# The last group of second experts, the slots' outputs, the combination and the output transfers by halves of the columns

## The chip, the cores and the metric

One Trainium2 chip, one of its cores. The metric is the device time of one execution in microseconds, the median of several runs.

## What is computed

Three layers in a row, all in float32 at the outside. Causal attention with a decay (4 x 8 heads, 576 rows, 64 columns), a mixture of 4 dense experts on the 2304 x 512 result, and a second, soft mixture, which the change touches:

```python
logits = x @ phi                       # 2304 x 32 slots
d = softmax of logits over the rows
slot_input = d.T @ x                   # 32 x 512, 8 experts of 4 slots
for e in range(8):
    h = np.maximum(slot_input[e] @ w1[e], 0.0)   # 4 x 1024
    slot_out[e] = h @ w2[e]                       # 4 x 512
c = softmax of logits over the slots
return c @ slot_out                    # 2304 x 512
```

## The kernel before, in words

Attention and the first mixture take the first 930 us or so. They stay as they are, instruction for instruction, and so does the order that the kernel's own scheduler makes of them. What follows is written out by hand, from L2096 on, in one straight line for all engines; each engine runs its own instructions in the order of the program.

The second experts are worked in two groups of four (`for g in range(NG2)`, L2158). Of a group, `ffn_in` (L2127) does the first layer, 1024 columns in two pieces of 512; `ffn_tr` (L2138) transposes; `ffn_out` (L2144) does the second layer: for each of eight blocks `m` of the inner dimension, the four experts write four strips of 32 partitions of one PSUM bank, `fo`. In the trace a float32 matmul is two rows, so a block `m` is eight. The weights come in through pages of SBUF: `fill` (L1837) starts the transfer of the next weights from SP into pages that are free, and `used` frees a page behind its matmul. The last weights are under way when group 1's second layer begins.

A group's result is scaled by the slots' totals on ScalarE into `so[g]` (L2175), and VectorE takes its largest magnitude (L2176). The slots' outputs are then `sel` times `so`: `sel[:, 0]` for group 0 (L2171, placed between the blocks of group 1) and `sel[:, 1]` for group 1 (L2183), summed in the bank `so`. For float16 they are scaled by a power of two that comes from the largest value of all: `spread` (L446) brings the 128 maxima of the partitions into every partition by a matmul, `top` (L449) takes the maximum of a row, two integer steps (L2188, L2190) make the power of two, ScalarE writes `SO` in float16 (L2192), VectorE puts the rounding rest into its lower half (L2193) and folds the scale into the factor of each row, `rc` (L2195).

Then the combination, for 18 tiles of 128 rows: one float16 matmul of 512 columns (L2199), an eviction with the factor of the row, by ScalarE for even tiles (L2204) and by VectorE for odd ones (L2202), and the transfer of 128 x 2 KB from SP (L2206). Tiles 4 and 13 hold 64 rows each of two sequences, so they go in two transfers of 64 rows: 20 in all. Each tile has a page of its own in SBUF.

Of the kernel before, what the change touches and what calls it, by code (L numbers as in the profile page):

```python
# [12 lines left out]
I32 = mybir.dt.int32  # L13
AF = mybir.ActivationFunctionType
ALU = mybir.AluOpType
AX = mybir.AxisListType
# [10 lines left out]
C_MUL = 1024.0  # L27
PAIRS = (0, 3, 3, 2)
PLAIN = (0, 1, 0, 0)
T_SO = 13  # L30
BIG = float(2 ** 23)
# [253 lines left out]
def moe_attention_kernel(ctx: ExitStack, tc: tile.TileContext, q, k, v, f, probs, w1, w2, phi, s1, s2, out):  # L285
    nc = tc.nc
    B, H, S, D = q.shape
    NT, DM = out.shape
# [4 lines left out]
    KD, KF = DM // 128, F // 128  # L293
    NTILE = NT // 128
# [10 lines left out]
    def page(p, n=1, dt=F32):  # L305
        a = arena[:, p * 512:(p + n) * 512]
        return a if dt is F32 else a.bitcast(dt)
# [63 lines left out]
    dyn = Pages(range(nxt[0], NPAGE))  # L371
# [25 lines left out]
    def rows(u):  # L397
        b, i = units[u]
        if i:
            return [(0, b * S + 64 + 128 * (i - 1), 128)]  # L400
        return [(0, b * S, 64), (64, (b + 1) * S, 64)]
# [43 lines left out]
    def spread(ps, col):  # L445
        nc.tensor.matmul(out=ps[:, 0:128], lhsT=col.to_broadcast([128, 128]), rhs=ident, start=True, stop=True)  # L446

    def top(dst, ps):
        nc.vector.tensor_reduce(out=dst, in_=ps[:, 0:128], axis=AX.X, op=ALU.max)  # L449
# [1207 lines left out]
    with tc.manual_schedule():  # L1657
# [65 lines left out]
        def bank(name):  # L1723
            if not ps2:
                return ps_m.tile([128, 512], F32, tag="m", name=name)
            return ps2[0].tile([128, 512], F32, tag="b", name=name)
# [25 lines left out]
        T = sc.task  # L1752
# [56 lines left out]
        sel = gp[:, E2 * 32:512].rearrange("p (g c) -> p g c", g=2)  # L1809
# [15 lines left out]
        NG2 = E2 // 4  # L1825
# [9 lines left out]
        where, held = {}, {}  # L1835

        def fill(keep=0):  # L1837

            ps = sorted(dyn.free_at, key=lambda p: (dyn.free_at[p], p))
            ps = sorted(ps[:max(0, len(ps) - keep)])  # L1840
            while ps and stream:
                ty, e2, n, kk = stream[-1]
                x = 1
                while (x < len(ps) and x < len(stream) and ps[x] == ps[0] + x
                       and stream[-1 - x] == (ty, e2, n, kk + x)):
                    x += 1
                if ty == "a":
                    src = s1[e2, kk * 128:(kk + x) * 128, n * 512:(n + 1) * 512]
                else:
                    src = s2[e2, kk * 128:(kk + x) * 128, :]  # L1850
                nc.sync.dma_start(out=page(ps[0], x).rearrange("p (k n) -> p k n", k=x),
                                  in_=src.rearrange("(k p) n -> p k n", p=128))
                for y in range(x):
                    key = stream.pop()
                    p = ps.pop(0)
                    where[key], held[key] = page(p), p
                    del dyn.free_at[p]

        def used(key):
            dyn.free(held.pop(key))  # L1860


        cT = page(dyn.alloc(3), 3, F16)[:, 0:NTILE * 128].rearrange("p (t c) -> p t c", c=128)
        x2T_p = dyn.alloc(3)
        x2T = page(x2T_p, 3).rearrange("p (k c) -> p k c", k=KD)
        mix = page(dyn.alloc(1))
# [4 lines left out]
        rc = mix[:, 404:404 + NTILE]  # L1871
        run_nm = [mix[:, 424:425], mix[:, 425:426]]
        run_sum = mix[:, 426:427]
        st_ = mix[:, 432:448]
# [132 lines left out]
        j = NBLK - 1  # L2007
# [61 lines left out]
        pm = bank("mg")  # L2069
# [19 lines left out]
        hs, so = page(hT_p, 2), [page(hT_p + 4), page(hT_p)]  # L2089
        hT = page(hT_p + 2, 2).rearrange("p (m c) -> p m c", m=KF)  # L2090
        SO = page(x2T_p + 2, 1, F16)[:, 0:DM]
# [4 lines left out]
        p = bank("sT")  # L2096
        for kk in range(KD):
            nc.tensor.matmul(out=p[:, kk * NS:(kk + 1) * NS], lhsT=slotS[R3, kk * 128:(kk + 1) * 128], rhs=G96[R3],
                             start=True, stop=True)
# [27 lines left out]
        def ffn_in(g, n, p, ks):  # L2127
            for kk in ks:
                for j in range(4):
                    key = ("a", 4 * g + j, n, kk)  # L2130
                    nc.tensor.matmul(out=p[32 * j:32 * j + 32, :], lhsT=slT[:, kk, 4 * g + j, :],  # L2131
                                     rhs=where[key], start=(kk == 0), stop=(kk == KD - 1))
                    used(key)
                fill(0)
            if ks[-1] == KD - 1:
                nc.scalar.activation(out=hs[:, n * 512:(n + 1) * 512], in_=p, func=AF.Relu)

        def ffn_tr(m0):  # L2138
            p = bank("hT")
            for m in range(4):  # L2140
                nc.tensor.transpose(p[:, m * 128:(m + 1) * 128], hs[:, (m0 + m) * 128:(m0 + m + 1) * 128], ident)
            nc.scalar.activation(out=hT[:, m0:m0 + 4, :], in_=p.rearrange("p (m c) -> p m c", m=4), func=AF.Copy)

        def ffn_out(g, p, ms):  # L2144
            for m in ms:
                for j in range(4):
                    key = ("b", 4 * g + j, 0, m)
                    nc.tensor.matmul(out=p[32 * j:32 * j + 32, :], lhsT=hT[:, m, 32 * j:32 * j + 32],  # L2148
                                     rhs=where[key], start=(m == 0), stop=(m == KF - 1))
                    used(key)  # L2150
                fill(0)

        def late():
            for x in tails.pop(0) if tails else ():
                x()

        pS = bank("so")
        for g in range(NG2):  # L2158
            ps = [bank("fh") for _ in range(NH)]
            ffn_in(g, 0, ps[0], range(KD))  # L2160
            late()
            ffn_in(g, 1, ps[1], range(KD // 2))
            ffn_tr(0)
            ffn_in(g, 1, ps[1], range(KD // 2, KD))
            p = bank("fo")
            ffn_out(g, p, range(2))
            ffn_tr(4)
            late()
            ffn_out(g, p, range(2, KF - 2))
            if g == NG2 - 1:  # L2170
                nc.tensor.matmul(out=pS, lhsT=sel[:, 0, :], rhs=so[0], start=True, stop=False)  # L2171
            ffn_out(g, p, range(KF - 2, KF))
            late()
            r = st_[:, 14 + g:15 + g]
            nc.scalar.activation(out=so[g], in_=p, func=AF.Copy, scale=r)  # L2175
            nc.vector.tensor_reduce(out=st_[:, 10 + g:11 + g], in_=so[g], axis=AX.X, op=ALU.max, apply_absolute_value=True)  # L2176
            if g == 0:
                nc.vector.tensor_scalar(out=st_[:, 10:11], in0=st_[:, 10:11], scalar1=float(2.0 ** -90), scalar2=None,
                                        op0=ALU.max)
                nc.vector.tensor_scalar(out=rc, in0=csum, scalar1=1e-9, scalar2=None, op0=ALU.add)  # L2180
                nc.vector.reciprocal(out=rc, in_=rc)
        p = pS
        nc.tensor.matmul(out=p, lhsT=sel[:, 1, :], rhs=so[1], start=False, stop=True)  # L2183
        nc.vector.tensor_tensor(out=st_[:, 11:12], in0=st_[:, 10:11], in1=st_[:, 11:12], op=ALU.max)
        pm = bank("mp")
        spread(pm, st_[:, 11:12])
        top(st_[:, 12:13], pm)
        nc.vector.tensor_scalar(out=st_[:, 12:13].bitcast(I32), in0=st_[:, 12:13].bitcast(I32), scalar1=0x7F800000,  # L2188
                                scalar2=None, op0=ALU.bitwise_and)
        nc.vector.tensor_scalar(out=st_[:, 13:14].bitcast(I32), in0=st_[:, 12:13].bitcast(I32), scalar1=-1.0,  # L2190
                                scalar2=(254 + T_SO) * BIG, op0=ALU.mult, op1=ALU.add)
        nc.scalar.activation(out=SO, in_=p, func=AF.Copy, scale=st_[:, 13:14])  # L2192
        nc.vector.scalar_tensor_tensor(out=SO[64:128], in0=p[64:128], scalar=st_[64:128, 13:14], in1=SO[64:128],  # L2193
                                       op0=ALU.mult, op1=ALU.subtract)
        nc.vector.tensor_scalar(out=rc, in0=rc, scalar1=st_[:, 12:13], scalar2=float(2.0 ** -T_SO) / C_MUL,  # L2195
                                op0=ALU.mult, op1=ALU.mult)
        for T in range(NTILE):
            p = bank("out")
            nc.tensor.matmul(out=p, lhsT=cT[:, T, :], rhs=SO, start=True, stop=True)  # L2199
            o = page(dyn.alloc(1))  # L2200
            if T % 2:
                nc.vector.tensor_scalar(out=o, in0=p, scalar1=rc[:, T:T + 1], scalar2=None, op0=ALU.mult)  # L2202
            else:
                nc.scalar.activation(out=o, in_=p, func=AF.Copy, scale=rc[:, T:T + 1])  # L2204
            for p0, r0, n in rows(T):
                nc.sync.dma_start(out=out[r0:r0 + n, :], in_=o[p0:p0 + n])  # L2206


DBG = {}
# [27 lines left out]
```

## Time and profile before

| | |
|---|---|
| median of 3 runs | 991.23 us (990.97 to 993.67) |
| profiled execution | 991.54 us |
| its span, first to last instruction | 989.8 us |
| instructions | 20653 |
| TensorE busy | 943.2 us, 95% |
| VectorE busy | 577.3 us, 58% |
| ScalarE busy | 471.9 us, 48% |
| GpSimd busy | 324.1 us, 33% |
| granted TensorE clock, mean | 0.992 |

Busy times are sums over the span; what a change at one place is worth is read at that place, in the chain that ended last and in the queues' own rows. The span leaves out the 1.7 us by which the execution's own time is longer.

### The profile page before, as it was taken

The numbers are of one execution on the slowest core, as the hardware profiler recorded it, in microseconds if no ns is written. First come the engines' busy times: TensorE is split into PE (matmuls) and PEld (weight loads), VectorE is DVE, ScalarE is ACT, GpSimd is POOL, SyncE is SP. The second block draws the span as 40 slices with busy tenths as digits, with TensorE's granted clock in tenths as the row PEclk, the third lists the DMA queues.
The fourth block names the chain that finished last, engine by engine and source line by source line (L and its number), as shares of the span: only waits on it lengthen the run. The fifth ranks groups of instructions, "written<-read, shape, count | busy, mean of one in ns | idle before, by whom it ended". The sixth has DMA issues, their size and how long they took to land.

```text
span 989.8 us, 20653 instructions
## 1 busy us (share of the span) xinstructions
PE 943.2 (95%) x8512; PEld 579.1 (59%) x8512; DVE 577.3 (58%) x1101; ACT 471.9 (48%) x1040; POOL 324.1 (33%) x316
## 2 busy tenths in 40 slices
PE   3998899999999999999999999999999999999994
PEld 2577787888878765455554545545454554555331
DVE  6979968886977398755256553315742353323313
ACT  6898878988887384252143612214431140111122
POOL 4997848874865298600004000000400000000000
PEclk9999999999999999999999999999999999999997
DMA  9658999999999510042002340000106113523695
GB/s 243 170 128 170 176 170 182 170 192 183 187 165 213 125 43 22 7 156 93 1 1 86 115 140 1 1 1 1 46 1 234 36 34 132 191 93 108 207 354 191
DMA packets 245247, 118.05 MB, mean 119 GB/s; under 512 B 217216, under 2 KB 217216, under 8 KB 245152
## 3 DMA queue, kind: packets, MB, share of 16 engines
q1 hardware_dynamic: 245104, 116.65, 48.1%
q8 instruction: 66, 1.08, 0.5%
q14 instruction: 29, 0.24, 0.1%
q10 hardware_dynamic: 48, 0.07, 0.0%
HBM read 73.58 MB, written 4.72 MB: 79 GB/s over the span
## 4 chain that ended last, share of the span: by engine, by line
PE 79%; DVE 10%; POOL 3%; issue 3%; ACT 3%; DMA 2%; SPq 0%; DVEq 0%; POOLq 0%; ACTq 0%
PE pso L876 25%; PE qA L785 11%; PE psh L588 7%; PE qE L785 6%; PE pso L609 6%; PE psh L631 3%; PE pso L649 3%; PE s L1260 3%; PE qF L785 3%; PE pv L1349 2%; DVE arena L438 2%; PE fh L2131 1%; PE fo L2148 1%; DMA arena<-arena 1%; PE qA L846 1%
## 5 line engine op out<-in xcount | busy, mean ns | idle before, releaser
L876 PE MATMUL pso<-arena 128*128 128x512 f16 x1152 | 255.1, 379 | 0.0
L876 PEld LDWEIGHTS <-arena 128*128 128x128 f16 x1152 | 112.4, 98 | 131.5 <-issue 1.2
L785 PEld LDWEIGHTS <-arena 128*128 128x128 f16 x1176 | 114.8, 98 | 80.5 <-issue 2.9
L536 POOL TENSOR_TENSOR arena<-arena 128x512 f32<-128x512 f32 x23 | 34.5, 1502 | 275.3 <-DVE arena L542 272.4
L785 PE MATMUL qA<-arena 128*128 128x384 f16 x672 | 121.1, 326 | 0.0
L655 DVE SCALAR_TENSOR_TENSOR arena<-pso,pw,arena 128x512 f32<-128x512 f32 x54 | 40.4, 748 | 126.1 <-PE pso L876 110.2
L588 PE MATMUL psh<-arena 128*128 128x128 f16 x1728 | 101.9, 219 | 2.1 <-DVE arena L1041 2.1
L609 PE MATMUL pso<-arena 128*128 128x512 f16 x432 | 98.8, 379 | 0.8 <-DVE arena L600 0.6
L588 PEld LDWEIGHTS <-arena 128*128 128x128 f16 x1728 | 97.3, 98 | 2.8 <-issue 2.2
L1301 ACT ACTIVATE arena<-s,mx,qs 128x320 f32<-128x320 f32 (+4 forms) x144 | 91.8, 646 | 2.4 <-POOL arena L1318 0.4
L1318 POOL TENSOR_TENSOR arena<-arena 128x512 f16<-128x512 f32 (+4 forms) x89 | 79.2, 911 | 17.9 <-ACT arena L1127 15.8
L808 ACT ACTIVATE arena<-qA 128x384 f32<-128x384 f32 x56 | 27.2, 486 | 116.6 <-PE qA L785 116.6
L1281 DVE TENSOR_REDUCE mx<-s 128x1 f32<-128x576 f32 (+4 forms) x76 | 64.1, 849 | 10.4 <-PE s L1260 10.2
L2087 POOL MEMSET arena<- 128x1024 f32 x1 | 1.0, 952 | 209.5 <-PE lg L1913 209.5
L1260 PE MATMUL s<-arena 128*128 128x128 f16 (+1 forms) x928 | 65.7, 213 | 1.5 <-ACT arena L1301 1.3
L609 PEld LDWEIGHTS <-arena 128*128 128x128 f16 x432 | 40.3, 98 | 44.7 <-issue 1.1
L785 PE MATMUL qE<-arena 128*128 128x384 f16 x336 | 63.7, 326 | 0.6 <-DVE arena L799 0.6
L693 POOL TENSOR_TENSOR arena<-arena 128x768 f32<-128x768 f32 (+2 forms) x27 | 54.3, 2025 | 26.3 <-DVE arena L693 22.8
L1260 PEld LDWEIGHTS <-arena 128*128 128x128 f16 x928 | 57.4, 98 | 2.5 <-issue 1.8
L1129 POOL TENSOR_SCALAR arena<-arena 128x576 f16<-128x576 f32 (+4 forms) x50 | 38.2, 767 | 53.1 <-ACT arena L1301 41.9
L542 DVE SCALAR_TENSOR_TENSOR arena<-arena,wm 128x512 f16<-128x512 f32 x46 | 52.0, 1166 | 4.2 <-ACT arena L539 4.2
L1349 PE MATMUL pv<-arena 128*128 128x64 f16 (+1 forms) x1312 | 49.7, 194 | 1.2 <-DMA arena<-arena 0.7
(235 smaller groups left out, 1480.5 us busy)
## 6 DMA issues: line engine op xcount, KB each, us to landing
arena<-in_moe_w_dram SPq DMA_DIRECT2D x57, 512.0 KB, 4.2
arena<-in_moe_w_dram SPq DMA_DIRECT2D x61, 256.0 KB, 5.1
arena<-in_moe_w_dram SPq DMA_DIRECT2D x7, 1024.0 KB, 7.0
arena<-in_moe_w_dram SPq DMA_DIRECT2D x7, 768.0 KB, 8.7
arena<-in_k_dram SPq DMA_DIRECT2D x16, 256.0 KB, 3.7
arena<-in_q_dram SPq DMA_DIRECT2D x16, 256.0 KB, 3.8
arena<-in_v_dram SPq DMA_DIRECT2D x16, 256.0 KB, 3.5
out_dram<-arena SPq DMA_DIRECT2D x16, 256.0 KB, 2.6
```

What stands on the lines that cost most here:

```text
L542: return lambda: nc.vector.scalar_tensor_tensor(out=wS[e][o][:, 1, c], in0=b, scalar=am[:, 7:8], in1=wS[e][o][:, 0, c], op0=ALU.mult, op1= ...
L588: nc.tensor.matmul(out=ps[:, m, :], lhsT=wt["w1" + a, 0][:, kk, ms], rhs=xT[j][:, b + kk, ts], start=(n == 0), stop=(n == 3 * KD - 1))
L609: nc.tensor.matmul(out=ops[u], lhsT=a[:, m, ts], rhs=wt["w2" + b, 0][:, m, :], start=(m == 0 and z == 0), stop=(m == KF - 1 and z == 2))
L655: nc.vector.scalar_tensor_tensor(out=acc[T], in0=ps, scalar=pw[:, e, T:T + 1], in1=acc[T], op0=ALU.mult, op1=ALU.add)
L693: return (LO, lambda eng: by[eng].tensor_tensor(out=at_(o), in0=at_(x), in1=at_(y), op=f), deps)
L785: nc.tensor.matmul(out=ps[c], lhsT=wS[e][o][:, y, k, ms], rhs=x[z][:, k], start=(first and i == 0), stop=(i == 5), skip_group_check=True)
L876: nc.tensor.matmul(out=cell[0], lhsT=a[:, m, ts], rhs=wt["w2" + b, e][:, m, :], start=(len(left) == KF - 1 and z == 0), stop=(not left and ...
L1260: nc.tensor.matmul(out=o, lhsT=qT[u][:, 2 * h + w, :], rhs=kT[kk][:, 2 * h + w, k0:k0 + n_], start=(w == 0), stop=(w == 1 and mask is None))
L1281: nc.vector.tensor_reduce(out=mx[:, 0:nh].rearrange("p (a h) -> p a h", a=sv.shape[1]), in_=sv, axis=AX.X, op=ALU.max, negate=True)
L1301: nc.scalar.activation(out=P[:, x], in_=sv[:, x // hb, x % hb], func=AF.Exp, scale=qs[u][:, 4:5], bias=mxs[n][:, 4 + x:5 + x], accum_out=s ...
L1318: by[eng].tensor_tensor(out=t[:, :, d0:d0 + n_], in0=P[:, :, s0:s0 + n_], in1=t[:, :, s0:s0 + n_], op=ALU.subtract)
L1349: nc.tensor.matmul(out=pv[u][r, h, :], lhsT=pt[:, w, r], rhs=rhs, start=(z == 0), stop=(z == len(mm) - 1))
```

## The change

In group 1 the second layer is done for columns 0 to 255 first, then for 256 to 511. `ffn_out` gets the columns as a parameter, and frees a weight's page only behind the second half. Behind the first half `group_out` evicts it and takes its maximum, together with that of the same half of group 0; `slots_1` and `biggest` do the slots' sum and the scaling for that half, placed between the blocks of the second half's second layer. Each half has its own maximum, its own power of two and its own factors `rch`. The combination is done for all 18 tiles and the first half, then for all tiles and the second; the second half's `slots_1` stands ahead of tile 1 and its `biggest` ahead of tile 4. A half tile has 256 columns: one matmul, one eviction (ScalarE even, VectorE odd, as before) and its transfer, rows of 1 KB, 40 transfers in all.

```diff
@@ -2141,20 +2141,74 @@
                 nc.tensor.transpose(p[:, m * 128:(m + 1) * 128], hs[:, (m0 + m) * 128:(m0 + m + 1) * 128], ident)
             nc.scalar.activation(out=hT[:, m0:m0 + 4, :], in_=p.rearrange("p (m c) -> p m c", m=4), func=AF.Copy)
 
-        def ffn_out(g, p, ms):
+        def ffn_out(g, p, ms, c=slice(0, DM)):
+
             for m in ms:
                 for j in range(4):
                     key = ("b", 4 * g + j, 0, m)
-                    nc.tensor.matmul(out=p[32 * j:32 * j + 32, :], lhsT=hT[:, m, 32 * j:32 * j + 32],
-                                     rhs=where[key], start=(m == 0), stop=(m == KF - 1))
-                    used(key)
+                    nc.tensor.matmul(out=p[32 * j:32 * j + 32, c], lhsT=hT[:, m, 32 * j:32 * j + 32],
+                                     rhs=where[key][:, c], start=(m == 0), stop=(m == KF - 1))
+                    if c.stop == DM:
+                        used(key)
                 fill(0)
 
         def late():
             for x in tails.pop(0) if tails else ():
                 x()
 
+
+        halves = [slice(x, x + DM // 2) for x in (0, DM // 2)]
         pS = bank("so")
+        rch = mix[:, 464:464 + 2 * NTILE].rearrange("p (h t) -> p h t", h=2)
+        mxs_ = mix[:, 448:464]
+
+        def group_out(g, c, h):
+            r = st_[:, 14 + g:15 + g]
+            nc.scalar.activation(out=so[g][:, c], in_=fo[g][:, c], func=AF.Copy, scale=r)
+            if h is None:
+                nc.vector.tensor_reduce(out=mxs_[:, 0:2], in_=so[g].rearrange("p (h c) -> p h c", h=2), axis=AX.X,
+                                        op=ALU.max, apply_absolute_value=True)
+                nc.vector.tensor_scalar(out=mxs_[:, 0:2], in0=mxs_[:, 0:2], scalar1=float(2.0 ** -90), scalar2=None,
+                                        op0=ALU.max)
+            else:
+                nc.vector.tensor_reduce(out=mxs_[:, 2 + h:3 + h], in_=so[g][:, c], axis=AX.X, op=ALU.max,
+                                        apply_absolute_value=True)
+                nc.vector.tensor_tensor(out=mxs_[:, 2 + h:3 + h], in0=mxs_[:, h:h + 1], in1=mxs_[:, 2 + h:3 + h],
+                                        op=ALU.max)
+
+        def slots_1(h):
+            nc.tensor.matmul(out=pS[:, halves[h]], lhsT=sel[:, 1, :], rhs=so[1][:, halves[h]], start=False, stop=True,
+                             skip_group_check=True)
+
+        def biggest(h):
+            pm = bank("mp")
+            spread(pm, mxs_[:, 2 + h:3 + h])
+            c, m, i = halves[h], mxs_[:, 4 + h:5 + h], mxs_[:, 6 + h:7 + h]
+            top(m, pm)
+            nc.vector.tensor_scalar(out=m.bitcast(I32), in0=m.bitcast(I32), scalar1=0x7F800000, scalar2=None,
+                                    op0=ALU.bitwise_and)
+            nc.vector.tensor_scalar(out=i.bitcast(I32), in0=m.bitcast(I32), scalar1=-1.0, scalar2=(254 + T_SO) * BIG,
+                                    op0=ALU.mult, op1=ALU.add)
+            nc.scalar.activation(out=SO[:, c], in_=pS[:, c], func=AF.Copy, scale=i)
+            nc.vector.scalar_tensor_tensor(out=SO[64:128, c], in0=pS[64:128, c], scalar=i[64:128], in1=SO[64:128, c],
+                                           op0=ALU.mult, op1=ALU.subtract)
+            nc.vector.tensor_scalar(out=rch[:, h], in0=rc, scalar1=m, scalar2=float(2.0 ** -T_SO) / C_MUL, op0=ALU.mult,
+                                    op1=ALU.mult)
+
+        def outputs(T, h):
+            c = halves[h]
+            p = bank("out")[:, c]
+            nc.tensor.matmul(out=p, lhsT=cT[:, T, :], rhs=SO[:, c], start=True, stop=True)
+            if h == 0:
+                o_pg[T] = page(dyn.alloc(1))
+            o = o_pg[T][:, c]
+            if T % 2:
+                nc.vector.tensor_scalar(out=o, in0=p, scalar1=rch[:, h, T:T + 1], scalar2=None, op0=ALU.mult)
+            else:
+                nc.scalar.activation(out=o, in_=p, func=AF.Copy, scale=rch[:, h, T:T + 1])
+            for p0, r0, n in rows(T):
+                nc.sync.dma_start(out=out[r0:r0 + n, c], in_=o[p0:p0 + n])
+        fo, o_pg = {}, {}
         for g in range(NG2):
             ps = [bank("fh") for _ in range(NH)]
             ffn_in(g, 0, ps[0], range(KD))
@@ -2162,48 +2216,35 @@
             ffn_in(g, 1, ps[1], range(KD // 2))
             ffn_tr(0)
             ffn_in(g, 1, ps[1], range(KD // 2, KD))
-            p = bank("fo")
-            ffn_out(g, p, range(2))
+            p = fo[g] = bank("fo")
+            c = halves[0] if g == NG2 - 1 else slice(0, DM)
+            ffn_out(g, p, range(2), c)
             ffn_tr(4)
             late()
-            ffn_out(g, p, range(2, KF - 2))
+            ffn_out(g, p, range(2, KF - 2), c)
             if g == NG2 - 1:
-                nc.tensor.matmul(out=pS, lhsT=sel[:, 0, :], rhs=so[0], start=True, stop=False)
-            ffn_out(g, p, range(KF - 2, KF))
+                nc.tensor.matmul(out=pS, lhsT=sel[:, 0, :], rhs=so[0], start=True, stop=False, skip_group_check=True)
+            ffn_out(g, p, range(KF - 2, KF), c)
             late()
-            r = st_[:, 14 + g:15 + g]
-            nc.scalar.activation(out=so[g], in_=p, func=AF.Copy, scale=r)
-            nc.vector.tensor_reduce(out=st_[:, 10 + g:11 + g], in_=so[g], axis=AX.X, op=ALU.max, apply_absolute_value=True)
             if g == 0:
-                nc.vector.tensor_scalar(out=st_[:, 10:11], in0=st_[:, 10:11], scalar1=float(2.0 ** -90), scalar2=None,
-                                        op0=ALU.max)
+                group_out(g, c, None)
                 nc.vector.tensor_scalar(out=rc, in0=csum, scalar1=1e-9, scalar2=None, op0=ALU.add)
                 nc.vector.reciprocal(out=rc, in_=rc)
-        p = pS
-        nc.tensor.matmul(out=p, lhsT=sel[:, 1, :], rhs=so[1], start=False, stop=True)
-        nc.vector.tensor_tensor(out=st_[:, 11:12], in0=st_[:, 10:11], in1=st_[:, 11:12], op=ALU.max)
-        pm = bank("mp")
-        spread(pm, st_[:, 11:12])
-        top(st_[:, 12:13], pm)
-        nc.vector.tensor_scalar(out=st_[:, 12:13].bitcast(I32), in0=st_[:, 12:13].bitcast(I32), scalar1=0x7F800000,
-                                scalar2=None, op0=ALU.bitwise_and)
-        nc.vector.tensor_scalar(out=st_[:, 13:14].bitcast(I32), in0=st_[:, 12:13].bitcast(I32), scalar1=-1.0,
-                                scalar2=(254 + T_SO) * BIG, op0=ALU.mult, op1=ALU.add)
-        nc.scalar.activation(out=SO, in_=p, func=AF.Copy, scale=st_[:, 13:14])
-        nc.vector.scalar_tensor_tensor(out=SO[64:128], in0=p[64:128], scalar=st_[64:128, 13:14], in1=SO[64:128],
-                                       op0=ALU.mult, op1=ALU.subtract)
-        nc.vector.tensor_scalar(out=rc, in0=rc, scalar1=st_[:, 12:13], scalar2=float(2.0 ** -T_SO) / C_MUL,
-                                op0=ALU.mult, op1=ALU.mult)
+        group_out(1, halves[0], 0)
+        ffn_out(1, p, range(2), halves[1])
+        slots_1(0)
+        ffn_out(1, p, range(2, 5), halves[1])
+        biggest(0)
+        ffn_out(1, p, range(5, KF), halves[1])
+        group_out(1, halves[1], 1)
         for T in range(NTILE):
-            p = bank("out")
-            nc.tensor.matmul(out=p, lhsT=cT[:, T, :], rhs=SO, start=True, stop=True)
-            o = page(dyn.alloc(1))
-            if T % 2:
-                nc.vector.tensor_scalar(out=o, in0=p, scalar1=rc[:, T:T + 1], scalar2=None, op0=ALU.mult)
-            else:
-                nc.scalar.activation(out=o, in_=p, func=AF.Copy, scale=rc[:, T:T + 1])
-            for p0, r0, n in rows(T):
-                nc.sync.dma_start(out=out[r0:r0 + n, :], in_=o[p0:p0 + n])
+            if T == 1:
+                slots_1(1)
+            if T == 4:
+                biggest(1)
+            outputs(T, 0)
+        for T in range(NTILE):
+            outputs(T, 1)
 
 
 DBG = {}
```

On SP, the end of the program, behind the three transposes of `cT`. Each row is a run of equal transfers to `out_dram`, 128 or 64 rows by 512 or 256 columns:

```order
 L1965 DMA_TRANSPOSE arena<-arena 128x1x128 x3
-L2206 DMA out_dram<-arena 128x512 x4
-L2206 DMA out_dram<-arena 64x512 x2
-L2206 DMA out_dram<-arena 128x512 x8
-L2206 DMA out_dram<-arena 64x512 x2
-L2206 DMA out_dram<-arena 128x512 x4
-L2232 UNCONDITIONAL_BRANCH
+L2210 DMA out_dram<-arena 128x256 x4
+L2210 DMA out_dram<-arena 64x256 x2
+L2210 DMA out_dram<-arena 128x256 x8
+L2210 DMA out_dram<-arena 64x256 x2
+L2210 DMA out_dram<-arena 128x256 x8
+L2210 DMA out_dram<-arena 64x256 x2
+L2210 DMA out_dram<-arena 128x256 x8
+L2210 DMA out_dram<-arena 64x256 x2
+L2210 DMA out_dram<-arena 128x256 x4
```

20 transfers became 40, of half the bytes each, in the order of the tiles, first halves ahead of second halves.

On VectorE, from the first half's scaling on (`so` is the slots' sum, `mp` the bank of the spread maxima, `out` a half tile):

```order
+L2193 SCALAR_TENSOR_TENSOR arena<-so,arena 64x256
 L2195 TENSOR_SCALAR arena<-arena 128x18
-L2202 TENSOR_SCALAR arena<-out,arena 128x512 x9
-L2232 UNCONDITIONAL_BRANCH
+L2174 TENSOR_REDUCE arena<-arena 128x1
+L2176 TENSOR_TENSOR arena<-arena 128x1
+L2206 TENSOR_SCALAR arena<-out,arena 128x256 x2
+L449 TENSOR_REDUCE arena<-mp 128x1
+L2188 TENSOR_SCALAR arena<-arena 128x1
+L2190 TENSOR_SCALAR arena<-arena 128x1
+L2193 SCALAR_TENSOR_TENSOR arena<-so,arena 64x256
+L2195 TENSOR_SCALAR arena<-arena 128x18
+L2206 TENSOR_SCALAR arena<-out,arena 128x256 x16
```

Two output evictions (tiles 1 and 3) now stand ahead of the second half's maximum and scaling, and the other sixteen behind it.

## Rows read from the trace of the kernel before

**Rows 1.** Chain that ended last, 959 to 980 us: start us, us, engine and line.
```profile
959.99 1.72 PE fo L2148 x16
961.71 0.59 PE hT L2141 x4
962.30 3.57 PE fo L2148 x32
965.87 1.06 PE so L2171 x2
966.92 1.95 PE fo L2148 x16
...
968.96 0.70 ACT arena L2175
...
973.50 4.96 PE out L2199 x14
```

**Rows 2.** Busy by stretch: engines us, granted clock, DMA share, GB/s.
```profile
5.00:10.00 5.00, 1.04 (x6) 0.94 (x7) 2.01 (x4) 4.83 (x14) 0.00 (x0) 1.00 1.09 248
...
966.00:975.40 9.40, 6.15 (x30) 1.89 (x30) 3.71 (x9) 2.87 (x5) 0.00 (x0) 0.97 0.00 0
...
975.50:988.00 12.50, 3.96 (x12) 1.20 (x9) 4.92 (x8) 4.06 (x7) 0.00 (x0) 0.64 1.01 376
...
976.00:978.00 2.00, 2.00 (x6) 0.70 (x5) 1.89 (x4) 1.71 (x3) 0.00 (x0) 0.50 1.06 409
```

**Rows 3.** Timeline, VectorE's last evictions, then SP's queue: start us, us, line, count.
```profile
978.48 2.07 DVE L2202 TENSOR_SCALAR arena<-out,arena 128x512 f32<-128x512 f32 x3
...
974.62 11.33 SPq L2206 DMA_DIRECT2D out_dram<-arena  x20
...
975.06 0.89 SPq L2206 DMA_DIRECT2D out_dram<-arena  x2
...
976.54 1.20 SPq L2206 DMA_DIRECT2D out_dram<-arena  x2
...
977.83 0.54 SPq L2206 DMA_DIRECT2D out_dram<-arena  x1
...
978.46 0.40 SPq L2206 DMA_DIRECT2D out_dram<-arena  x1
...
979.96 0.69 SPq L2206 DMA_DIRECT2D out_dram<-arena  x1
...
985.49 0.46 SPq L2206 DMA_DIRECT2D out_dram<-arena  x1
```

**Rows 4.** Line 2206: issue times in ns, min/median/max, and times to landing.
```profile
L2206 SPq DMA_DIRECT2D out_dram<-arena x20: 342/488/686, 974.6 to 985.5; - x20
...
DMA to landing us min/median/max: 2.0/2.6/3.0
```

**Rows 5.** SP's waits, 935 to 990 us: total us, times, longest us.
```profile
SPq L2232 <- DMA out_dram<-arena: 2.4, 2, 1.8
```

**Rows 6.** Last weight issue on SP; weight transfers issued in 935 to 960 us.
```profile
959.02 0.33 SPq L1851 DMA_DIRECT2D arena<-in_moe_w_dram  x1
...
arena<-in_moe_w_dram SPq DMA_DIRECT2D x34, 256.0 KB, 5.7
```

**Rows 7.** Groups by line and shape: busy us, mean ns; the first from the page.
```profile
L808 ACT ACTIVATE arena<-qA 128x384 f32<-128x384 f32 x56 | 27.2, 486 | 116.6 <-PE qA L785 116.6
...
L2202 DVE TENSOR_SCALAR arena<-out,arena 128x512 f32<-128x512 f32 x9 | 6.3, 747 | 0.5 <-PE out L2199 0.4
...
L2175 ACT ACTIVATE arena<-fo,arena 128x512 f32<-128x512 f32 x1 | 0.7, 688 | 6.0 <-PE fo L2148 6.0
...
L2176 DVE TENSOR_REDUCE arena<-arena 128x1 f32<-128x512 f32 x1 | 0.7, 686 | 14.2 <-ACT arena L2175 14.2
...
L2136 ACT ACTIVATE arena<-fh 128x512 f32<-128x512 f32 x1 | 0.6, 598 | 1.4 <-PE fh L2131 1.4
...
L449 DVE TENSOR_REDUCE arena<-mp 128x1 f32<-128x128 f32 x1 | 0.3, 292 | 0.6 <-PE mp L446 0.6
```

## The prediction

> **What bounds the kernel now.** I read the chain of waits first, since only the end of the program is touched. [rows 1] show TensorE on the chain through the second group's second layer (1.72, 3.57 and 1.95 us of `fo`, with 1.06 us of the slot matmul between), and then, from 968.96 us, a strictly serial piece: eviction (0.70), slot matmul, the maximum over the partitions, the scaling to float16, and only at 973.50 us the first output matmul. The reader should see 4.5 us there (968.96 to 973.50) in which TensorE has almost nothing to do, and before it that the chain is all matmul.
>
> The chain view stops with the last evictions, but the span ends at 989.8. So I read the stretches next: the DMA engines do nothing from 966 to 975.4 and are then at a mean share of 1.01 until 988 [rows 2]. The last 14 us are the output's way out. The third view is SP's queue [rows 3]: 20 transfers are issued between 974.62 and 985.95, one behind the other. VectorE's last three evictions end at 980.55 (978.48 + 2.07); from there every output tile lies ready in SBUF, and SP is still issuing for 5.4 us. The last issue starts at 985.49 and takes 0.46; after it the closing lines wait 2.4 us in all for the output [rows 5], to 988.4, so that transfer took 2.9 us; 1.4 us of closing follow.
>
> So two limits lie on top of each other: bytes (18 tiles of 256 KB) and SP's issues. The question is which one the change moves, since it halves the size of a transfer and doubles their number.
>
> **The early part of the change.** The first half of `fo` takes half the columns, so half of 1.72, 3.57 and 1.95 us: 3.6 us. With the transposes (0.59) and the slot matmul (1.06), which stay whole, the first half ends at 965.3 from its start at 959.99. Next in line is the weights' arrival: the last of them is issued at 959.02, and such a transfer lands after a median of 5.7 us [rows 6], at 964.7; the last two rows of blocks then need 0.43 us or a little more. I take 965.4, against 968.87 before: 3.5 us earlier.
>
> The chain behind it, with durations for 256 columns. ScalarE has 0.49 us at 384 columns and 0.60 at 512 [rows 7], 0.11 for 128 columns, so the scaled 0.69 becomes about 0.46. VectorE's maximum takes 0.29 at 128 columns and 0.69 at 512, 1.03 ns a column; so 256 columns take 0.42, and its passes of 0.75 out of PSUM become 0.48. First half: eviction to 965.9, maximum and comparison to 966.55, all behind TensorE's second-half matmuls, which run meanwhile; TensorE reaches the spread of the maximum after five of eight rows at 968.5; VectorE's three small steps to 969.2, scaling to 969.7 and 970.2, reciprocal scale to 970.5. The first output tile leaves ScalarE at 971.0 and SP issues it there, 3.6 us earlier than 974.62.
>
> But only four half tiles (T = 0 to 3) precede the second half's scaling on ScalarE and VectorE. Both engines run in order, so tile 4 waits behind it. The second half's sums end on TensorE at 969.8, its maximum on VectorE at 971.1; VectorE evicts tiles 1 and 3 first (2 x 0.48), then takes the maximum and its two small steps to 972.7; scaling to 973.2 on ScalarE. Tile 4 leaves ScalarE at 973.7 and I put its first issue at **973.8**. The four early issues fit in the hole before. What the change adds beside this (a second set of the chain's small instructions, 32 more second-layer matmuls of half the width, a second spread, 18 more evictions) I cost at nothing, since SP covers it: from tile 4 on, ScalarE and VectorE have 16 half tiles each at about 0.48 us, 7.7 us, ending near 981.5. Without that cover, were SP free, this is the next bound. TensorE's output matmuls stand on the chain with 4.96 us for 14 tiles [rows 1], 0.35 a tile; halves have as many columns in all.
>
> **SP's issues.** From tile 4 on, 36 transfers are left: 28 of 128 rows, 8 of 64 rows (tiles 4 and 13 lie across two sequences, in both halves). What one costs on SP is the term that decides. The trace has no transfer of 128 x 1 KB, so I bound it. An issue took 342 to 686 ns [rows 4], and the time to the next start is what counts. The first four starts, when the queue is empty, are 0.48 us apart on average (974.62 to 976.54). Three steps in the middle are 0.50 each (978.46 to 979.96). The whole 20 are 0.572 apart (974.62 to 985.49, 19 steps). The two of 64 rows, half the bytes, are no shorter: 0.645 apart (976.54 to 977.83, two steps). A half tile resembles those most in bytes and the empty queue most in load. That 64 rows cost as much as 128 says that an issue is priced by the piece and not by the byte. I take 0.48 for 128 rows, the empty queue, and 0.645 for 64 rows. Bounds: 0.44 for every one (the first step, 974.62 to 975.06) and 0.572 for every one.
>
> Is the drain slower than that? Time of a packet on its engine is size x 16 x share / rate: 256-byte pieces at 248 GB/s and share 1.09 take 18 ns, 2 KB pieces at 409 GB/s and 1.06 take 85 ns [rows 2]. A line through both gives 47 ns for 1 KB (an estimate from these rows), 8 x 47 = 0.37 us for a half tile on 16 engines. That is less than 0.48, so SP is the bound and the DMA engines fall idle between transfers.
>
> Sum: 35 steps from tile 4's first issue to the last are 27 x 0.48 + 8 x 0.645 = 13.0 + 5.1 = 18.1 us, so the last issue starts at 991.9 where it started at 985.49. Without a backlog I give its landing the shortest one seen, 2.0 us [rows 4], for 2.9; closing 1.4 as before. Span 973.8 + 18.1 + 2.0 + 1.4 = **995.3**, against 989.8: **5.5 us longer**. The profiled execution took 991.54 us, 0.3 above the median of 991.23; so 991.54 + 5.5 = **997.0 us**. By the bounds: 35 x 0.44 = 15.4 gives 994.3; 35 x 0.572 = 20.0, with a landing of 2.6, gives 999.5.
>
> On this the trace and a rule differ. Rows: after 980.55 us nothing but SP's issues, a half microsecond and more each, precedes the transfers. The Trainium skill, in "DMA: Bandwidth & Descriptors", section "Issuing engines are not separate DMA queues", says that the time an issuing engine needs to start a DMA is usually small beside the DMA itself. By it the sum would be that of the first rival, below; no run here yet has small output transfers, and 0.48 against 0.37 speaks the other way.
>
> **Rivals.**
>
> 1. *The DMA queue sets the pace, not SP* (not slower). The issue times of 0.40 to 0.69 us may be SP held back by a full queue: the engines are at a share near 1 all the while [rows 2], and landing stays at 2.0 to 3.0 us [rows 4], as with a short queue that pushes back. Then smaller transfers issue faster, and the early start counts. 32 half tiles from 974.7 (0.9 us after the issue, as from 974.62 to 975.5 before) at 0.37 are 11.9 us, drained at 986.6, where the engines went quiet at 988.0: 1.4 us gained, 990.1 us; at the full rate of 2 KB pieces 2.4 gained, 989.1 us. It decides if an issue of 1 KB rows takes under 0.37 us. Against it: the shortest step is 0.44 with an empty queue, and the 64-row transfers would have to be short. Chance 0.12.
>
> 2. *A 1 KB row costs the engines as much as a 2 KB row.* Then a half tile takes 0.68 us to drain, the four early ones are out by 974.6, and 32 x 0.68 = 21.8 us end at 996.4, 8.4 later than 988.0: 999.9 us. For it: only two sizes fix my line. Against: both ends of it scale with bytes. Chance 0.08.
>
> 3. *SP as forecast, but at the low bound* (0.44 a step, also for 64 rows): 994.3 us. This is the lower edge of the forecast and not another case.
>
> **How the numbers follow.** Forecast 0.76, rival 1 0.12, rival 2 0.08, the rest unnamed. A measurement of this kernel can tell about 0.3%, 3.0 us, from no change: below 988.2 is faster, above 994.2 slower. Nothing that I could work out passes 988.2, since even with no cost of halving 3.6 us of earlier start are mostly spent waiting for tile 4; I leave 0.03. Within 0.3%: rival 1, and the low edge of the forecast if tile 4 comes before 973.8: 0.18. Slower: 0.79. The range of 8 in 10 leaves out rival 1 and a little at the top: 993.5 to 999.5.
>
> **What would show it.** In the changed profile: SP's first output issue near 971, a short gap, then 36 issues with no wait between them to about 992; steps of 0.48 us and of 0.6 for 64 rows; a DMA share below 0.85 after 974; compute over by 982. It is wrong if the issues shrink towards 0.37 us with the share still near 1 (rival 1), or if the share stays at 1 while landings grow past 3 us (rival 2). If the first issue comes no earlier than 974, the early part has failed and the loss is larger.

## The result, and the profile after

| | before | after |
|---|---|---|
| median | 992.05 us (6 runs) | 1001.40 us (6 runs) |
| ratio, 95% interval | | 1.0087 (1.0076 to 1.0098) |
| profiled execution, its span | 991.54, 989.8 us | 1001.33, 999.6 us |

The change makes the kernel 0.9% slower. The forecast was 997.0 us, with a range to 999.5: the direction held, the size did not.

The timeline of the changed kernel, from the start of the second experts on (start us, us, engine, line, operation, output and inputs; in brackets the idle time before and what ended it):

```profile
937.85 1.07 PE L2131 MATMUL fh<-arena 128*32 128x512 f32 x8
...
968.41 0.47 ACT L2167 ACTIVATE arena<-fo,arena 128x256 f32<-128x256 f32 x1 [3.41 <-PE fo L2149]
...
968.94 1.07 PE L2149 MATMUL fo<-arena 128*32 128x256 f32 x16 [0.71 <-ACT arena L2167]
...
970.57 1.50 PE L2149 MATMUL fo<-arena 128*32 128x256 f32 x24
...
972.00 0.49 PE L446 MATMUL mp<-ident,arena 128*128 128x128 f32 x2
...
975.14 22.16 SPq L2210 DMA_DIRECT2D out_dram<-arena  x40
...
977.21 7.34 ACT L2208 ACTIVATE arena<-out,arena 128x256 f32<-128x256 f32 x16
...
978.14 6.87 DVE L2206 TENSOR_SCALAR arena<-out,arena 128x256 f32<-128x256 f32 x16
```

The second experts start at 937.85 us here, at 935.04 in the profile before. No instruction ahead of that place differs; I count from that start in both, and come back to the 2.8 us below. From there to the end of the span it is 61.75 us after the change and 54.8 before: **7.0 us more in the part that was changed**. The first output tile is issued at 975.14, 37.3 us after that start, where it was 39.6 before (974.62 in [rows 3]): 2.3 us were won. Then SP issues for 22.16 us where it issued for 11.33.

SP's queue in the changed kernel, single issues (start us, us): tile 4's first, two in the middle, four about tile 13, and the last:

```profile
977.71 0.56 SPq L2210 DMA_DIRECT2D out_dram<-arena  x1
...
980.63 0.41 SPq L2210 DMA_DIRECT2D out_dram<-arena  x1
...
981.13 0.41 SPq L2210 DMA_DIRECT2D out_dram<-arena  x1
...
983.14 0.47 SPq L2210 DMA_DIRECT2D out_dram<-arena  x1
...
983.66 0.59 SPq L2210 DMA_DIRECT2D out_dram<-arena  x1
...
984.34 0.54 SPq L2210 DMA_DIRECT2D out_dram<-arena  x1
...
984.97 0.41 SPq L2210 DMA_DIRECT2D out_dram<-arena  x1
...
996.90 0.41 SPq L2210 DMA_DIRECT2D out_dram<-arena  x1
```

Issue line 2210 as a whole, in ns, and its times to landing:

```profile
L2210 SPq DMA_DIRECT2D out_dram<-arena x40: 332/410/588, 975.1 to 996.9; - x40
...
DMA to landing us min/median/max: 1.7/1.8/2.0
```

The busy time by stretch (stretch, length, PE, PEld, DVE, ACT, POOL, granted clock, DMA share, GB/s):

```profile
978.00:980.00 2.00, 1.62 (x10) 0.77 (x8) 1.97 (x6) 1.82 (x6) 0.00 (x0) 1.00 0.31 83
980.00:982.00 2.00, 1.63 (x10) 0.86 (x9) 2.00 (x6) 1.85 (x5) 0.00 (x0) 1.00 0.75 262
992.00:994.00 2.00, 0.00 (x0) 0.00 (x0) 0.00 (x0) 0.00 (x0) 0.00 (x0) 0.50 0.75 262
```

Read together: an issue takes 410 ns in the median, and the next one starts 0.50 us after it (980.63, 981.13), though nothing holds it up: transfers land within 1.7 to 2.0 us, less than in [rows 4], the DMA engines are busy for 0.75 of the time where only 128-row transfers go out, and for less elsewhere (0.31 about tile 4's two transfers of 64 rows), where [rows 2] have 1.06, and from 985 us on every tile lies ready (978.14 + 6.87). A pair of 64 rows (983.14, 983.66) and the transfer behind it stretch three steps to 1.83 us. SP's issues are the bound.

### The profile page after: what moved, and what is told of

It reads as the page before. It is cut to its first block, busy times and chain, and to the rows that moved or that the text cites. A ratio compares the mean times of both kernels' runs of the same rounds, so it can differ in the third digit from the quotient of the medians.

```text
span 999.6 us, 20891 instructions
## 1 busy us (share of the span) xinstructions
PE 946.7 (95%) x8598; PEld 583.1 (58%) x8598; DVE 581.5 (58%) x1117; ACT 472.9 (47%) x1051; POOL 321.0 (32%) x316
## 4 chain that ended last, share of the span: by engine, by line
PE 78%; DVE 9%; issue 3%; ACT 3%; POOL 3%; DMA 2%; SPq 0%; DVEq 0%; POOLq 0%; ACTq 0%
PE pso L876 25%; PE qA L785 11%; PE psh L588 6%; PE pso L609 6%; PE qE L785 5%; PE psh L631 3%; PE pso L649 3%; PE s L1260 3%; PE qF L785 3%; PE pv L1349 2%; DVE arena L438 2%; PE fh L2131 1%; PE fo L2149 1%; DMA arena<-arena 1%; PE qA L846 1%
```

## The experiments

Theory S: each output transfer has a price on SP's queue, about 0.50 us, that hardly depends on its size, and 40 of them are longer than the drain (the time that the DMA engines need for the bytes). Rival C: the loss comes from the halved second layer, its waits and the second scaling. Rival D: rows of 1 KB are what hurts, in the engines or the memory. "Start" below is that of the second experts in the same profile; a ratio is to the kernel before in the same set of runs, with its 95% interval.

**The transfers alone.** In the kernel before:

```diff
-            for p0, r0, n in rows(T):
-                nc.sync.dma_start(out=out[r0:r0 + n, :], in_=o[p0:p0 + n])
+            for c in (slice(0, DM // 2), slice(DM // 2, DM)):
+                for p0, r0, n in rows(T):
+                    nc.sync.dma_start(out=out[r0:r0 + n, c], in_=o[p0:p0 + n, c])
```

> The kernel before, with the output transfers alone cut into column halves: two per tile (rows of 1 KB), 40 in all; the compute is untouched. Theory S (SP's issue per transfer is the bound, 0.50 us a step for 128 rows and 0.6 for 64, as in the changed kernel): last issue starts 32 x 0.50 + 8 x 0.6 - 0.5 = 20.3 us after the first, where before it was 10.9; the shorter landing gives back 1.6, so about 7.8 us longer than before, near 1000 us. Rival C (the loss comes from the halved second layer, its waits and the second scaling): no more than the slower drain of 1 KB rows, 4608 x 46 ns / 16 = 13.2 us for 12.2, near 993.

Measured: 1002.18 us against 993.57, ratio 1.0086 (1.0068 to 1.0104), as much as the whole change. The timeline, first row of the second experts and SP's issues, and the issue line:

```profile
937.63 0.64 PE L2131 MATMUL fh<-arena 128*32 128x512 f32 x4
...
977.21 21.49 SPq L2207 DMA_DIRECT2D out_dram<-arena  x40
```

```profile
L2207 SPq DMA_DIRECT2D out_dram<-arena x40: 347/452/602, 977.2 to 998.3; - x40
...
DMA to landing us min/median/max: 1.7/1.8/2.1
```

The first issue is where it was before, 39.6 us after the start; SP then issues for 21.49 us, and the end comes 63.4 us after the start, 8.6 more than before. Rival C falls: with the compute untouched the loss is there.

**The compute alone.** The changed kernel with its halves, but each tile sent whole, once both halves are evicted (`if h == 1`, rows of 2 KB); `biggest(1)` stands ahead of the tiles' second halves, and from tile 4 on the two halves of a tile follow each other.

> The changed kernel with whole-tile transfers (20, rows of 2 KB): the second half's scaling stands ahead of the tiles' second halves, each tile is evicted in two halves and sent once. The halved compute stays. Theory S: the first issue comes when both halves are scaled, about 1.2 us later than in the kernel before (counted from the start of the second experts), then the same 20 steps: about 993. Rival C: stays near 1001, since all of the halved compute is still there.

Measured: 994.24 us against 993.57, ratio 1.0011 (1.0001 to 1.0021). Start and SP:

```profile
936.27 1.07 PE L2131 MATMUL fh<-arena 128*32 128x512 f32 x8
...
977.23 11.30 SPq L2211 DMA_DIRECT2D out_dram<-arena  x20
```

20 issues in 11.30 us, as before; they begin 41.0 us after the start for 39.6, and the end comes 56.1 us after it for 54.8. So the halved chain delays the point where both halves are scaled by 1.4 us, and with 20 transfers in place of 40 the rest of the loss is gone.

**A bank of its own.** In the timeline above TensorE idles for 0.71 us at 968.94, until ScalarE has read the first half: the second half's matmuls write the same PSUM bank.

```diff
+        p = bank("fo2")
         ffn_out(1, p, range(2), halves[1])
...
+        fo[1] = p
         group_out(1, halves[1], 1)
```

> The changed kernel with a PSUM bank of its own for the second half of the second layer. In the changed kernel TensorE idles 0.71 us ahead of the second half's first matmul until ScalarE has evicted the first half. Theory S: this idle time goes, everything behind it comes 0.7 us earlier, and since SP issues without a pause from tile 4 on, the end too: about 1000.7. Rival: SP's start does not matter because the engines' drain or evictions decide: end unchanged.

Measured: 999.96 us, ratio 1.0067 (1.0052 to 1.0082) against 1.0087 with the shared bank. TensorE, then SP:

```profile
937.34 1.06 PE L2131 MATMUL fh<-arena 128*32 128x512 f32 x8
...
966.74 1.93 PE L2149 MATMUL fo<-arena 128*32 128x256 f32 x32
968.61 0.70 PE L2180 MATMUL so<-arena 128*128 128x256 f32 x2
...
973.82 22.17 SPq L2210 DMA_DIRECT2D out_dram<-arena  x40
```

The second layer's two halves now run as one row of 32 with no idle time. First issue 36.5 us after the start for 37.3, end 61.0 for 61.75: the 0.8 us go through to the end, as they must where SP's issues are the last chain. By time alone the two kernels are not told apart (the intervals overlap); the trace shows it.

**Two queues.** The changed kernel, odd tiles from tile 5 on issued by ScalarE:

```diff
-            if T % 2:
+            if T % 4:
...
+            q = nc.scalar if T % 2 and (h or T > 4) else nc.sync
             for p0, r0, n in rows(T):
-                nc.sync.dma_start(out=out[r0:r0 + n, c], in_=o[p0:p0 + n])
+                q.dma_start(out=out[r0:r0 + n, c], in_=o[p0:p0 + n])
```

> The changed kernel with the odd tiles' transfers, from tile 5 on, issued from ScalarE (18) and the rest from SP (22); VectorE evicts three tiles of four so that ScalarE has time. Theory S: SP is through about 22 x 0.53 = 11.6 us after its first issue, ScalarE after 10 x 0.46 + 18 x 0.5 = 13.6 us from the second scaling, so the last issue is near 991 in the changed kernel's time where it was 996.9: about 995.5. Rival D (the DMA engines or HBM bound 1 KB rows): no gain, and a share near 1 with landing times well over 2 us.

Measured: 995.37 us, ratio 1.0019 (1.0009 to 1.0028). The issue line by queue, and two stretches:

```profile
L2211 SPq DMA_DIRECT2D out_dram<-arena x22: 332/405/585, 973.7 to 989.0; - x22
...
L2211 ACTq DMA_DIRECT2D out_dram<-arena x18: 338/388/613, 977.7 to 988.6; - x18
...
DMA to landing us min/median/max: 1.7/2.4/2.8
...
982.00:984.00 2.00, 1.78 (x7) 0.84 (x7) 1.85 (x5) 1.41 (x3) 0.00 (x0) 0.50 0.97 323
986.00:988.00 2.00, 0.07 (x1) 0.00 (x0) 0.60 (x2) 0.47 (x1) 0.00 (x0) 1.00 1.02 350
```

The end comes 56.2 us after the start for 61.75. Same 40 transfers, same packets, same bytes; with two issuers the engines' share goes from 0.75 to about 1 (323 to 350 GB/s), landing grows to 2.4 us, and the time falls. Rival D falls as the cause of the 7 us: the engines can drain rows of 1 KB at that rate, and are the next bound once they are issued fast enough.

**Fewer issues, same packets.** The changed kernel with a bank of its own and two neighbouring half tiles in one transfer:

```diff
+            elif T > first:
+                r0 = rows(first)[0][1]
+                nc.sync.dma_start(out=out[r0:r0 + 256, c].rearrange("(t p) c -> p t c", p=128), in_=o_two[first][:, :, c])
```

> The changed kernel, second half of the second layer in a bank of its own, with the half tiles of two neighbouring tiles sent in one transfer of 256 rows (still rows of 1 KB; tiles 4 and 13 as before): 24 issues for 40, the same packets and bytes, the same computing. Theory S: from tile 4 on 22 issues of 0.5 to 0.6 us, 12.5 us; or, if that is less, the drain of 1 KB packets, 32 half tiles x 0.37 us and some for the 64-row ones, also about 12.5: last issue 51 us after the start of the second experts, end near 54.5 (changed kernel 61.7, before 54.8); ratio 0.999 to 1.001. Rival D (1 KB rows, not the issues): stays near 1.007.

Measured: 994.93 us against 993.29, ratio 1.0017 (1.0008 to 1.0026). The start, SP's first two issues and six later ones, the line of the 256-row transfers, and three stretches:

```profile
936.83 1.06 PE L2131 MATMUL fh<-arena 128*32 128x512 f32 x8
...
973.97 0.90 SPq L2220 DMA_DIRECT2D out_dram<-arena  x2
...
977.07 2.15 SPq L2220 DMA_DIRECT2D out_dram<-arena  x4
979.32 1.12 SPq L2217 DMA_DIRECT2D out_dram<-arena  x2
...
L2220 SPq DMA_DIRECT2D out_dram<-arena x16: 372/443/527, 974.0 to 988.5; - x16
...
DMA to landing us min/median/max: 2.1/2.4/2.8
...
978.00:980.00 2.00, 1.63 (x10) 0.87 (x10) 2.00 (x6) 1.85 (x5) 0.00 (x0) 1.00 1.00 351
982.00:984.00 2.00, 0.38 (x2) 0.00 (x0) 1.01 (x3) 0.62 (x2) 0.00 (x0) 1.00 1.09 384
986.00:988.00 2.00, 0.00 (x0) 0.00 (x0) 0.00 (x0) 0.00 (x0) 0.00 (x0) 0.60 1.08 381
```

24 issues for 40 take the end from 61.0 us (same kernel, single half tiles) to 55.2 us after the start. An issue of 256 rows costs 443 ns, where 128 rows cost 410: the price hangs on the issue. Two limits lie close together here: the engines are at a share of 0.83 to 1.09 in the stretches of 2 us from 978 to 990, and SP still issues one behind another (four and two in the rows at 977.07 and 979.32, with 0.1 us between). The first issue, 37.1 us after the start, is 2.4 us earlier than in the kernel before, and the end still 0.4 later. An estimate for the engines: the packets of 1 KB (47 ns each by 0.75 x 16 x 1024 / 262 GB/s in the changed kernel's rows) need 4608 x 47 / 16 = 13.5 us, where 2304 of 2 KB at 85 ns [rows 2] need 12.2.

The same with the eight 64-row transfers on ScalarE's queue:

> As a_pairs, with the eight transfers of 64 rows issued from ScalarE and the sixteen of 256 rows from SP. SP then has 14 issues of 0.5 to 0.6 from tile 5 on, 8 us, and is the bound no more; the drain of 1 KB packets is (near 12.5 us from tile 4 on): end 53.5 to 54.5 us after the start of the second experts. If two queues feed the engines better while 64-row packets take twice as long, up to 1 us earlier than a_pairs.

Measured: 994.07 us, ratio 1.0009 (1.0001 to 1.0018), end 55.0 us after the start. The gain of up to 1 us did not come: 0.1.

```profile
out_dram<-arena SPq DMA_DIRECT2D x16, 256.0 KB, 3.1
...
982.00:984.00 2.00, 1.53 (x6) 0.54 (x5) 1.52 (x4) 0.53 (x3) 0.00 (x0) 0.50 1.04 360
988.00:990.00 2.00, 0.00 (x0) 0.00 (x0) 0.00 (x0) 0.00 (x0) 0.00 (x0) 0.50 1.08 378
```

With SP relieved of eight issues, the 256-row transfers land 3.1 us after their issue in the median, where it was 2.4, and the share is 1.04 and 1.08: now the engines are the bound, and that is where the gain ends.

**Is the kernel before bound by its issues too?** Its tiles in pairs of 512 KB, 12 issues for 20:

> The kernel before with two tiles in one transfer of 512 KB (12 issues for 20). If the drain bounds the kernel before (2304 packets of 84 ns over 16 engines, 12.1 us): data end within 0.5 us of the 53.0 us after the start of the second experts, a first transfer 0.4 us later, ratio 1.000. If its 20 issues bound it (0.57 us a step): up to 1 us faster, 0.999.

Measured: 993.74 us, ratio 1.0009 (0.9998 to 1.0020), end 54.5 us after the start for 54.8.

```profile
L2215 SPq DMA_DIRECT2D out_dram<-arena x8: 394/490/1058, 976.3 to 985.7; - x8
...
DMA to landing us min/median/max: 2.7/3.7/5.0
...
984.00:986.00 2.00, 0.00 (x0) 0.00 (x0) 0.00 (x0) 0.00 (x0) 0.00 (x0) 0.50 1.05 404
```

With half the issues the time stays, the share is 1.05, and landing grows to 3.7 us: the backlog lies in the engines. The kernel before is bound by its drain, and its 0.57 us a step were close behind. Those 0.57 us are not SP's price alone: an issue takes up to 1.06 us here while landing grows to 5.0, so SP is held back where the engines are behind.

**Halves by rows.** The kernel before, 36 transfers of 64 rows x 2 KB:

> The kernel before with every output transfer cut by rows: 36 of 64 rows, rows of 2 KB; the compute is untouched. Theory S (a price for each issue, and 64 rows dearer than 128): 35 steps of 0.6 are 21 us where 19 steps took 10.9, near 9 us longer, about 1002, although the packets are as large as before. If small packets were what hurt (rival D): no change, 993.5.

Measured: 1004.57 us against 993.45, ratio 1.0107 (1.0089 to 1.0125); end 65.7 us after the start, 10.9 more than before.

```profile
L2207 SPq DMA_DIRECT2D out_dram<-arena x36: 474/570/602, 977.2 to 999.9; - x36
...
DMA to landing us min/median/max: 2.2/2.3/2.4
...
980.00:982.00 2.00, 1.87 (x7) 0.56 (x5) 1.90 (x4) 1.86 (x4) 0.00 (x0) 0.85 0.90 208
990.00:992.00 2.00, 0.00 (x0) 0.00 (x0) 0.00 (x0) 0.00 (x0) 0.00 (x0) 0.50 0.87 205
```

The cost is somewhat above what was expected, but this run does not part the theories as I thought. The share is 0.87 to 0.90 at 205 GB/s: a packet of 2 KB takes 2048 x 16 x 0.87 / 205 = 139 ns, where whole tiles have 85 [rows 2]. So 64-row transfers load the engines more per byte, and their 0.6 us a step may be drain as well as issue.

**The start of the second experts.** The changed kernel and the kernel before once more:

> The changed kernel once more, to part what lies ahead of the second experts from what lies behind. From the start of their first layer to the end the changed kernel took 61.75 us, the kernel before 54.77, 7.0 more; their starts were 937.85 and 935.04 us, 2.8 apart. If that start only scatters from execution to execution, the ratio comes near 1.0070 (7.0 us); if the change itself delays the start, 1.0099.

> The kernel before, unchanged, for a second profile. If the start of the second experts scatters: between 935 and 938 us here too, and 54.8 us from there to the end. If the changed kernel alone starts late: 935.0 again.

Measured: ratio 1.0078 (1.0060 to 1.0095), 1000.67 us against 993.45; from the start to the end 61.7 and 54.8 us, the same as in the first profiles to 0.1. The starts were 937.61 and 936.61. Over all 13 profiles they lie between 935.04 and 937.85, and the first profile of the kernel before is the earliest of all. The kernel before alone moved by 1.6 us between its two profiles, so most of the 2.8 us is scatter of the part that was not changed. The five profiles with 36 or 40 transfers on SP's queue start at 937.3 to 937.9 (mean 937.6), the other eight at 935.0 to 937.8 (mean 936.6). For four of those five the medians differ from the kernel before's by 0.0 to 0.3 us more than the profiles do from the start on; only the table above, with six runs each, has 9.35 us for 7.0. Whether the change has a share of some tenths in the start stays open.

**A version that keeps the early start.** Bank of its own; column halves sent for tiles 0 to 3 only, the rest whole:

> The changed kernel with the halved chain kept (second half of the second layer in a bank of its own), but column halves sent only for tiles 0 to 3, whose first halves go while the second half is being scaled; tiles 4 to 17 are evicted after both scalings and sent whole: 24 issues. Theory S: 20 issues are left at the second scaling, 39.3 us from the start of the second experts, where the kernel before has 20 from 39.6; 0.5 MB less to drain. End 0.5 to 1.5 us before the kernel before's 54.8, ratio 0.9985 to 0.9995, not to be told from 1 by time, but in the trace. If the early start is lost in a new wait: 1.000 or above.

Measured: 995.09 us, ratio 1.0016 (1.0007 to 1.0025), end 55.5 us after the start, 0.7 behind the kernel before. A miss. SP, its first issue behind the second scaling, and two stretches:

```profile
974.17 15.04 SPq L2212 DMA_DIRECT2D out_dram<-arena  x24
...
977.73 0.33 SPq L2212 DMA_DIRECT2D out_dram<-arena  x1
...
978.00:980.00 2.00, 2.00 (x6) 0.76 (x5) 1.63 (x5) 1.80 (x6) 0.00 (x0) 0.50 0.56 197
984.00:986.00 2.00, 0.00 (x0) 0.00 (x0) 0.39 (x1) 0.00 (x0) 0.00 (x0) 1.00 1.06 407
```

When the second scaling is done, SP has 20 issues left, as the kernel before has, but the first of them comes 39.9 us after the start (977.73) and not 39.3, 0.4 later than the kernel before's first, and four of them carry half a tile each: the engines sit at a share of 0.56 (978 to 980) where SP's price, not the bytes, sets the pace, and only later reach 1.06. How the 0.7 us divide between the two, no run shows. No version here beats the kernel before by time.

## Why the prediction was right and wrong

Right: SP's issues bound the changed kernel; 0.50 us a step against 0.37 for the drain of a half tile decided it, and with a second issuer the end came 5.5 us earlier. The Trainium skill ("DMA: Bandwidth & Descriptors", "Issuing engines are not separate DMA queues") says that issuing from several engines saves only the time to initiate the DMA, usually small beside the DMA itself. The first half agrees with the run with two queues. The second is not so for transfers of 128 KB here, which take SP 0.41 us to issue, 0.50 from start to start, and the engines 0.37 to drain; the measurement decides. Rival 1 (issues shrink when the queue is empty) had its premise right and its size wrong: the median issue went from 488 ns [rows 4] to 410 when the backlog was gone, but not under the 370 that it needed; the step stayed at 0.50 us and the share fell to 0.75 and less. Rival 2 did not happen: a 1 KB packet took 47 ns by the rows above, as my line gave. Tile 4 waited for the second scaling and the four early issues fitted ahead of it, as forecast.

Wrong was the size, from the start of the second experts 7.0 us for 5.5 (1.1 + 1.1 - 0.7 in the first three points), and the range's top:

- *Tile 4's first issue* was put at 973.8, 38.8 us after the start; it came at 39.9 (977.71), 1.1 late; the first tile, put at 971.0 or 36.0 us, came at 37.3. The step that failed is "all behind TensorE's second-half matmuls, which run meanwhile": those waited 0.71 us for the eviction of the first half out of the same bank. I had read that chain for durations and not for who else uses the bank. The rest is the half-width matmuls: 24 rows take 1.43 us from 970.57 to the next spread (972.00 in the same timeline), 60 ns each for 54 forecast, which makes 0.4 us for the 64 rows of the second half.
- *The steps*: 35 were put at 18.1 us and took 19.2 (977.71 to 996.90). "I take 0.48, the empty queue" was the wrong row. An empty queue gives 0.43 to 0.48 only to the first issues behind a pause; back to back it is 0.50, the three steps of [rows 3] that I had named and not taken. And I priced a pair of 64 rows at two steps of 0.645, while it is three steps that stretch: the transfer behind a pair is dear too. One pause of 0.43 us between two issues (987.39 to 987.82), whose cause no run shows, is in the 19.2 as well.
- *Landing and closing* were put at 3.4 and took 2.7: 128 KB without backlog lands in 1.8, which I had bounded by the 2.0 of a whole tile, and the closing took 0.9 where I had kept 1.4. Here I was lucky: it hid 0.7 us of the loss.
- *The base*: I added the difference to one profiled execution (991.54), near a median of three runs (991.23). Later sets of 17 to 29 runs of the kernel before have medians of 993.3 to 993.6. That the part ahead scatters by 2.8 us was not in my range; 7.0 us on 992.05 would be 999.05, within it, and 1001.4 is not. What scatters there, no run shows.

## What to carry to other kernels

A transfer has two prices, bytes on the engines and, here, about half a microsecond on the queue that issues it; cut a transfer only as long as the drain of a piece stays longer than its issue. A whole tile still met that (0.68 us against 0.50), a half tile did not (0.37), so halving made the issue the bound at once. When an earlier start is bought with smaller pieces, work out the time to the last piece, and not to the first. Before a chain is overlapped with the matmuls behind it, look at which bank those write. And a difference between two profiled executions is counted from a common place just ahead of the change.

## What the runs showed that I had not expected

A transfer of 64 rows is dear in the engines, not only on the queue: 139 ns for a 2 KB packet against 85 when 128 rows go at once, 205 GB/s at a share of 0.87. Transfers of 256 rows by 1 KB cost SP 443 ns, hardly more than 128 rows.

TensorE's granted clock stayed at 1.00 (the 2.4 GHz level) from 980 to 982 us in the changed kernel, while it was at 0.50 (1.2 GHz) from 976 to 978 in the kernel before [rows 2], both with output matmuls running, of 256 columns in the one and 512 in the other. Ahead of them TensorE had little to do from 968.96 to 973.50 in the kernel before [rows 1], and worked through the second half in the changed one. The version with column halves for four tiles alone, in which TensorE waits for the second scaling without work, shows 0.50 from 978 to 980. But work ahead did not keep the clock up: with a bank of its own TensorE goes through the second half without the 0.71 us of idle time, and the output matmuls of the changed kernel run at 0.50 there:

```profile
980.00:982.00 2.00, 1.73 (x8) 0.82 (x7) 1.56 (x4) 1.75 (x4) 0.00 (x0) 0.50 0.75 261
```

What decided it stays open. It made no difference to the end, which SP set: 22.17 us of issues in that kernel, 22.16 in the changed one.
